# A filter fold that reads its mirrored half by a negative step, and a new fixed order of work

## The chip, the cores and the metric

The kernel runs on one core of one Trainium2 chip. The metric is the device time of one execution in microseconds (us), the median over repeated runs; the smaller the better. Besides it there is a profile of one execution of the kernel before: every instruction with its start and duration on each engine, what it waited for, and the transfers.

The engines by their short names: PE is TensorE (matmul), PEld its weight loads, DVE is VectorE, ACT is ScalarE, POOL is GpSimd, SP is SyncE, which issues most transfers. PE writes its results into PSUM, which has eight banks of 512 columns of 32 bits; DVE or ACT read them from there.

## What is computed

A gated sum of two branches over S = 2048 tokens of D = 640 features, all in bfloat16 at the borders:

```python
def _A_ref(q, k, v, shift_k, ssm_k, ssm_D):
    k_shift = sum of four shifted copies of k, each times its tap of shift_k
    kv = k_shift * v
    y = causal convolution of kv with the filters ssm_k, S long, by FFT over 2 * S
    y = y + kv * ssm_D
    return q * y

def _B_ref(x, w1, w2, w3, w4):
    h = gelu(layernorm(x) @ w1)
    hs = (quarters of h shifted by +1, -1, +2, -2 tokens) @ w2
    x1 = x + hs
    return x1 + gelu(layernorm(x1) @ w3) @ w4

x = A_q
g = sigmoid((x * gate_w).sum(-1, keepdims=True))
return g * _A_ref(x, A_k, A_v, ...) + (1 - g) * _B_ref(x, ...)
```

The code above is shortened to what each line computes.

## The kernel before

**Stages.** Tokens are the 16 tiles of 128 (t), or four chunks of 512 (sc). Branch B: `ln1` normalises the tiles of x and transposes them (tiles 0 to 7 by PE and an ACT copy, the others by a transposing transfer), `mm1` multiplies by w1 and applies Gelu on ACT, `mm2` multiplies by w2 and adds x, `ln2` normalises again and transposes, `mm3` multiplies by w3 with Gelu, `mm4` by w4. Branch A works on two halves of the features (g or hh) and four blocks of tokens (b or c): `kv_half` and `kv_block` make the products of k, taps and v on DVE and fold them, `x_fwd` takes their folded transform on PE, `h_load`, `h_fold` and `h_chunk` do the same for the filters in five chunks of 128 features, `unit` multiplies the spectra on DVE, and `final` transforms back, in 16 steps that are numbered k = 0 to 15 (first the eight of one half, then those of the other). Each `final` step has an inverse transform on PE, a copy on ACT, an addition and a subtraction on DVE, a flip of the difference by a matmul, a copy of the flipped half on ACT scaled by the gate, a product with q on DVE, and an output transfer, which either adds into memory (by POOL's queue) or is issued by SP after one more addition on DVE.

**The fold of the filters** (`h_fold`, L765 to L774). The real transform of 512 values needs the sums and the differences of value n and value 512 - n. `kst` holds four blocks of 512 values per feature. Before, ACT copies values 511 to 257 in reversed order into `krev` (L769), whose first column holds zeros (L708); DVE subtracts and adds 256 columns of four blocks (L770, L771) and puts value 256 into column 0 of the sums (L772). Two transposing transfers follow (L773), and `h_chunk` uses their results as matmul operands.

**The order of work.** The program first records all operations in a list (`P.op`, `P.dma`), with what each reads and writes; the number of an operation is its place there, 0 to 1300. `SEQUENCE` (L502) lists these numbers in the order in which they are to be issued; filtered by engine it is each engine's program. `schedule` (L271) goes through it with planned durations, gives each PSUM tile the bank that comes free first by that plan, and lets large transfers wait for an earlier transfer that the plan has finished. `emit` (L322) then places the semaphore waits that the data and the banks need. An engine works strictly in its list's order, so an instruction that waits holds up everything behind it on its engine.

**Lines that the profile names.** Helpers record most operations, so many have one line: L689 is every matmul of `mm`, L669 every two-operand instruction of `tt`, L674 every `ts` (a tensor with one or two scalars), L679 every `act`, L861 POOL's power in the layernorms, L857 and L858 the statistics of `ln1`, L903 the PE transposes of `ln1`, L237 every transfer. L715 is a row of 15 matmuls on ones that warms PE up at the start. L718 is one Gelu of a single column whose result nobody reads. L737 copies the parts of w1 for the last feature tile (w1x) and needs both halves of w1, which SP loads by two transfers (L733 to L735; operations 34 and 35). `ln2` of a tile runs POOL, POOL, DVE, POOL (the power), DVE in turn.

Of the kernel before, what the change touches and what calls it, by code (L numbers as in the profile page):

```python
# [173 lines left out]
class Prog:  # L174
# [96 lines left out]
    def schedule(self, sequence, backlog=3000.0):  # L271
        ops = self.ops
        delays = self.edges()
        free = {"pe": 1580.0, "act": 720.0, "dve": 930.0, "pool": 1190.0, "sp": 720.0}
        dfree = 0.0
        done = []
        avail = [0.0] * 8
        tenant = [None] * 8
        todo = {t.idx: len(t.users) for t in self.banks}
        last = {t.idx: 0.0 for t in self.banks}  # L280
        order = []
        for i in sequence:
            o = ops[i]
            st = max([free[o.eng]] + [ops[p].end + d for p, d in delays[i]])
            if o.nbytes and not o.tp and not o.early:
                st = max(st, dfree - backlog)
            t = o.tile
            if t is not None and t.place is None:
                free_at = {b: max(avail[b:b + t.n]) for b in range(0, 8, t.n)}
                st = max(st, min(free_at.values()))  # L290
                assert st < 1e17, "no bank"
                t.place = min((avail[b ^ 1] <= st if t.n == 1 else False, a, b) for b, a in free_at.items() if a <= st)[2]
                for b in range(t.place, t.place + t.n):
                    if tenant[b] is not None:
                        for u in tenant[b].users:
                            if ops[u].eng != "pe":
                                o.preds.setdefault(u, False)
                    tenant[b] = t
                    avail[b] = 1e18
            o.start = st  # L300
            free[o.eng] = st + o.dur
            o.end = st + o.dur
            if o.nbytes:
                dfree = max(st + 0.5 * o.dur, dfree) + o.cost
                o.end = max(dfree, o.end) + o.lat
                if o.cost > 500 and not o.tp and not o.early:
                    gate = [(ops[d].end, d) for d in done if ops[d].end <= st]
                    if gate:
                        o.preds.setdefault(max(gate, key=lambda g: g[0])[1], False)
                done.append(i)  # L310
            if t is not None:
                todo[t.idx] -= 1
                last[t.idx] = max(last[t.idx], o.end)
                if todo[t.idx] == 0:
                    for b in range(t.place, t.place + t.n):
                        avail[b] = last[t.idx] + 195.0
# [147 lines left out]
def bass_gated_mix__ssm_conv_h3__mixer_s_mlp__prompt_kernel(  # L464
# [33 lines left out]
    def ps(n, cls):  # L498
# [3 lines left out]
    SEQUENCE = [2, 3, 10, 11, 12, 31, 6, 57, 8, 1, 13, 14, 15, 16, 17, 18, 19, 20, 21, 22, 23, 24, 25, 7, 9, 0, 4, 28, 5, 56, 29, 63, 58, 64,  # L502
# [684 lines left out]
```

## Time and profile before

| what | value |
|---|---|
| time, median of 3 runs | 236.11 us (235.93 to 236.24) |
| span of the profiled execution, first to last instruction | 233.8 us |
| what lies around the span, against the median | 2.3 us |
| PE busy | 221.1 us |
| DVE busy | 220.1 us |
| ACT busy | 170.3 us |
| POOL busy | 105.9 us |

The profiled execution's own time is its span and the few microseconds around it, in which the execution is started and ended. A row of the profile's groups reads: line, engine, operation, what it writes and reads with partitions x elements, the count; then busy us and the mean ns of one; then the engine's idle time just before these instructions and what ended most of it. In the timeline the first two numbers are the start and the time taken, and a bracket gives the idle time ahead and what ended it. In the chain of waits each row is a start, a duration, and the engine and line that the end of the program was waiting for at that time.

### The profile page before, as it was taken

What the parts mean: (1) busy time and instruction counts of PE and PEld (TensorE: products, weight loads), DVE (VectorE), ACT (ScalarE), POOL (GpSimd) and SP (SyncE); (2) the same over time, 40 slices, a digit from 0 to 9 for tenths busy, and PEclk for the clock granted to TensorE, in tenths of its full rate; (3) what the DMA queues carried; (4) which work ended last, traced back from release to release, by engine and by line L of the source; (5) the groups of instructions that cost most, each with busy time, mean ns of one, the idle gap of its engine ahead of it and who ended that gap; (6) DMA issues with size and microseconds to landing.
All of it is one profiled execution on the core that took longest, in us unless ns stands there. A gap on an engine that the chain in (4) does not pass through costs nothing.

```text
span 233.8 us, 4171 instructions
## 1 busy us (share of the span) xinstructions
PE 221.1 (95%) x1501; PEld 134.6 (58%) x1501; DVE 220.1 (94%) x402; ACT 170.3 (73%) x317; POOL 105.9 (45%) x122
## 2 busy tenths in 40 slices
PE   7999999989998999999999999999999999999960
PEld 2598665436554656544775456654666556776630
DVE  6998999999988999998999999999989999979994
ACT  2799699488796899769949897577655387288881
POOL 0330406274495801196376693246024332456870
PEclk9999999999999999999999999999999999999997
DMA  5999959898878999978638988999978987989998
GB/s 161 360 345 250 253 146 271 246 277 204 140 181 176 240 213 317 343 212 180 157 97 145 187 189 163 146 191 206 259 142 145 196 140 142 185 98 111 95 109 165
DMA packets 63785, 45.48 MB, mean 195 GB/s; under 512 B 28818, under 2 KB 59028, under 8 KB 63764
## 3 DMA queue, kind: packets, MB, share of 16 engines
q1 hardware_dynamic: 54748, 33.33, 55.2%
q0 software_dynamic: 8832, 11.80, 34.9%
q8 instruction: 12, 0.20, 0.3%
q10 hardware_dynamic: 184, 0.08, 0.1%
q14 instruction: 9, 0.07, 0.1%
HBM read 24.22 MB, written 6.55 MB: 132 GB/s over the span
## 4 chain that ended last, share of the span: by engine, by line
PE 45%; DVE 9%; POOL 3%; ACT 2%; issue 1%
PE PSall L689 45%; DVE arena L669 8%; ACT arena L679 2%; POOL arena L674 1%; POOL arena L861 1%; POOL arena L669 1%; DVE arena L959 0%; DVE arena L674 0%
## 5 line engine op out<-in xcount | busy, mean ns | idle before, releaser
L689 PE MATMUL PSall<-arena 128*128 128x320 bf16 (+5 forms) x1444 | 213.7, 307 | 5.3 <-DVE arena L669 2.4
L669 DVE TENSOR_TENSOR arena<-arena 128x640 bf16<-128x640 bf16 (+5 forms) x247 | 182.3, 793 | 3.0 <-ACT arena L679 1.9
L689 PEld LDWEIGHTS PSall<-arena 128*128 128x128 bf16 (+1 forms) x1444 | 130.5, 98 | 86.9 <-DVE arena L669 4.2
L679 ACT ACTIVATE arena<-PSall 128x512 bf16<-128x512 f32 (+6 forms) x189 | 107.7, 634 | 29.4 <-PE PSall L689 25.2
L679 ACT ACTIVATE arena<-arena 128x640 bf16<-128x640 bf16 (+4 forms) x62 | 42.2, 703 | 6.7 <-POOL arena L669 2.7
L861 POOL TENSOR_TENSOR arena<-arena 128x1 f32<-128x1 f32 (+1 forms) x26 | 29.3, 1128 | 31.9 <-DVE arena L674 31.5
L674 POOL TENSOR_SCALAR arena<-arena 128x1 f32<-128x1 f32 (+2 forms) x41 | 24.8, 608 | 34.7 <-DVE arena L959 12.0
L237 POOL DMA_DIRECT2D out_dram<-arena x28 | 30.5, 1197 | 20.5 <-ACT arena L679 15.0
L679 ACT ACTIVATE arena<-PSall,arena 128x640 bf16<-128x640 f32 (+1 forms) x32 | 20.6, 658 | 20.0 <-PE PSall L689 19.9
L237 POOL DMA_DIRECT2D arena<-arena x12 | 14.9, 1242 | 32.1 <-DVE arena L669 28.2
L674 DVE TENSOR_SCALAR arena<-arena 128x640 bf16<-128x640 bf16 (+2 forms) x49 | 14.4, 307 | 3.4 <-POOL arena L674 1.6
L857 DVE BATCH_NORM_STATS2 arena<-arena 128x6 f32<-128x320 bf16 x32 | 14.6, 479 | 2.0 <-DMA arena<-in_A_q_dram 1.7
L669 POOL TENSOR_TENSOR arena<-arena 128x1 f32<-128x1 f32 (+1 forms) x11 | 10.3, 943 | 2.9 <-DVE arena L674 2.5
L715 PE MATMUL PSall<-arena 128*128 128x512 bf16 x15 | 5.4, 536 | 1.6 <-DVE arena L711 1.6
L959 DVE SCALAR_TENSOR_TENSOR arena<-PSall,arena 128x640 bf16<-128x640 f32 x8 | 6.4, 808 | 0.1
L924 DVE TENSOR_SCALAR arena<-arena 32x256 bf16<-32x256 bf16 (+1 forms) x24 | 5.9, 244 | 0.5
L679 ACT ACTIVATE PSall<-PSall 128x640 f32<-128x640 f32 x8 | 5.6, 699 | 0.1
L715 PEld LDWEIGHTS PSall<-arena 128*128 128x128 bf16 x15 | 1.9, 132 | 4.6 <-issue 2.5
L903 PE MATMUL PSall<-arena 128*128 128x128 bf16 x40 | 3.6, 219 | 0.3
L718 ACT ACT_TABLE_LOAD x1 | 1.3, 1283 | 2.7 <-issue 2.7
L903 PEld LDWEIGHTS PSall<-arena 128*128 128x128 bf16 x40 | 2.4, 97 | 1.4 <-DVE arena L858 0.4
L858 DVE BATCH_NORM_AGGREGATE arena<-arena 128x2 f32<-128x12 f32 x16 | 3.0, 197 | 0.0
(24 smaller groups left out, 9.6 us busy)
## 6 DMA issues: line engine op xcount, KB each, us to landing
arena<-arena POOLq DMA_DIRECT2D x12, 640.0 KB, 6.3
arena<-in_A_k_dram SPq DMA_DIRECT2D x14, 400.0 KB, 4.1
arena<-in_A_q_dram SPq DMA_DIRECT2D x14, 320.0 KB, 6.9
out_dram<-arena POOLq DMA_DIRECT2D x20, 160.0 KB, 4.2
arena<-in_A_ssm_k_dram SPq DMA_DIRECT2D x5, 512.0 KB, 4.4
arena<-in_A_v_dram SPq DMA_DIRECT2D x16, 160.0 KB, 3.9
arena<-in_B_w_dram SPq DMA_DIRECT2D x1, 1920.0 KB, 8.8
out_dram<-arena SPq DMA_DIRECT2D x10, 160.0 KB, 3.7
```

What stands on the lines that cost most here:

```text
L237: fn = lambda e: e.dma_start(out, in_, **kw)
L669: P.op(eng, lambda e: e.tensor_tensor(o, real(a), real(b), op), [a, b], [o], dve_ns(o, [a, b], 2) if eng == "dve" else 500)
L674: P.op(eng, lambda e: e.tensor_scalar(o, real(a), s1, s2, op0=op0, **({} if op1 is None else {"op1": op1})), [a] + aps, [o], dve_ns(o, [a] ...
L679: P.op("act", lambda e: e.activation(real(o), real(a), f, bias=bias, scale=scale, **({"accum_out": accum} if accum is not None else {})), ...
L689: fns.append(lambda e, l=l, r=r, i=i: e.matmul(real(o), l, r, start=(i == 0), stop=(i == last)))
L715: P.op("pe", lambda e: e.matmul(real(pw), warm[:, 0:128], warm[:, 128:640], start=True, stop=True), [warm], [pw], 427.0 if i < 14 else 216.0)
L857: P.op("dve", lambda e, o=o, i=i: e.bn_stats(o, i), [i], [o], 400)
L858: P.op("dve", lambda e: e.bn_aggr(bna[:, t, :], bns[k]), [bns[k]], [bna[:, t, :]], 120)
L861: P.op("pool", lambda g: g.tensor_tensor(o, a, e, ALU.pow), [a, e], [o], dur)
L903: P.op("pe", [lambda e, c=c, pb=pb, xn=xn: e.transpose(real(pb)[:, 128 * c:128 * (c + 1)], xn[:, 128 * c:128 * (c + 1)], ident) for c in r ...
L924: P.op("dve", lambda e, o=hT[q, 4, c0:c0 + n], i=hx[q, :]: e.tensor_scalar(o, i, 1.0, None, op0=ALU.mult), [hx[q, :]], [hT[q, 4, c0:c0 + n ...
L959: P.op("dve", lambda e: e.scalar_tensor_tensor(x, real(pr), 1.0, x, op0=ALU.mult, op1=ALU.add, accum_out=st[1, 0][:, t:t + 1]), [pr, x], [ ...
```

## The change

`h_fold` loses its ACT copy and the buffer `krev` with its two zero fills. DVE's subtraction and addition now read `k[:, :, 511:256:-1]`, the same memory with a step of -1, and cover columns 1 to 255 of each block; one instruction copies values 256 and 0 into column 0 of sums and differences. The operations number 1294 instead of 1301, so numbers in the new lists are up to seven lower than before for the same operation.

The order is a new one throughout. `schedule` no longer plans with durations: `PLACES` gives the bank of each of the 230 PSUM tiles, and `GATES` lists 63 pairs of operations, of which the first waits for the second. The planned duration of a DVE instruction with a negative step is no longer set apart (`dve_ns`), but the new `schedule` doesn't use planned durations.

The diff, with most of the lists cut. Operations that the text below names are, before and after: the one-column Gelu 26 and 24; the halves of w1 34 and 35, now 32 and 33; the second load of x tiles 4 to 7 142, now 140; ln2 of token tile 3 on DVE 441 and 443, now 434 and 436; subtraction and product of output step 2 1159 and 1162, now 1152 and 1155, and of output step 0 1137 and 1140, now 1130 and 1133.

```diff
@@ -268,52 +268,23 @@
             out.append(row)
         return out
 
-    def schedule(self, sequence, backlog=3000.0):
+    def schedule(self, sequence, places, gates):
         ops = self.ops
-        delays = self.edges()
-        free = {"pe": 1580.0, "act": 720.0, "dve": 930.0, "pool": 1190.0, "sp": 720.0}
-        dfree = 0.0
-        done = []
-        avail = [0.0] * 8
         tenant = [None] * 8
-        todo = {t.idx: len(t.users) for t in self.banks}
-        last = {t.idx: 0.0 for t in self.banks}
         order = []
+        for d, g in gates:
+            ops[d].preds.setdefault(g, False)
         for i in sequence:
             o = ops[i]
-            st = max([free[o.eng]] + [ops[p].end + d for p, d in delays[i]])
-            if o.nbytes and not o.tp and not o.early:
-                st = max(st, dfree - backlog)
             t = o.tile
             if t is not None and t.place is None:
-                free_at = {b: max(avail[b:b + t.n]) for b in range(0, 8, t.n)}
-                st = max(st, min(free_at.values()))
-                assert st < 1e17, "no bank"
-                t.place = min((avail[b ^ 1] <= st if t.n == 1 else False, a, b) for b, a in free_at.items() if a <= st)[2]
+                t.place = places[t.idx]
                 for b in range(t.place, t.place + t.n):
                     if tenant[b] is not None:
                         for u in tenant[b].users:
                             if ops[u].eng != "pe":
                                 o.preds.setdefault(u, False)
                     tenant[b] = t
-                    avail[b] = 1e18
-            o.start = st
-            free[o.eng] = st + o.dur
-            o.end = st + o.dur
-            if o.nbytes:
-                dfree = max(st + 0.5 * o.dur, dfree) + o.cost
-                o.end = max(dfree, o.end) + o.lat
-                if o.cost > 500 and not o.tp and not o.early:
-                    gate = [(ops[d].end, d) for d in done if ops[d].end <= st]
-                    if gate:
-                        o.preds.setdefault(max(gate, key=lambda g: g[0])[1], False)
-                done.append(i)
-            if t is not None:
-                todo[t.idx] -= 1
-                last[t.idx] = max(last[t.idx], o.end)
-                if todo[t.idx] == 0:
-                    for b in range(t.place, t.place + t.n):
-                        avail[b] = last[t.idx] + 195.0
             o.order = len(order)
             order.append(o)
         return order
@@ -499,70 +470,88 @@
-    SEQUENCE = [2, 3, 10, 11, 12, 31, 6, 57, 8, 1, 13, 14, 15, 16, 17, 18, 19, 20, 21, 22, 23, 24, 25, 7, 9, 0, 4, 28, 5, 56, 29, 63, 58, 64,
-                59, 27, 141, 30, 60, 35, 61, 52, 65, 62, 76, 66, 26, 80, 67, 34, 77, 42, 68, 78, 70, 146, 53, 82, 69, 71, 43,
-                44, 46, 83, 79, 48, 50, 73, 81, 142, 321, 72, 47, 144, 301, 74, 75, 96, 205, 98, 86, 97, 84, 39, 87, 36, 143,
...
-                677, 655, 660, 647, 623, 441, 442, 702, 289, 290, 291, 292, 704, 652, 276, 424, 653, 656, 414, 443, 284, 705,
...
-                1187, 1075, 1108, 1061, 1173, 1110, 1107, 1079, 1120, 1158, 1159, 1143, 1160, 1161, 1132, 1174, 1076, 1137,
-                1080, 1138, 1139, 1149, 1062, 1177, 1178, 1109, 1162, 1111, 1140, 1070, 1081, 1150, 1188, 1189, 1125, 1163,
...
+    SEQUENCE = [1, 6, 27, 8, 9, 10, 0, 2, 11, 12, 13, 55, 28, 61, 62, 63, 66, 67, 57, 78, 29, 14, 15, 54, 58, 59, 16,
+                77, 25, 60, 56, 71, 64, 17, 79, 18, 139, 141, 19, 20, 72, 21, 22, 23, 26, 73, 40, 41, 42, 33, 144,
+                82, 140, 50, 51, 145, 75, 3, 44, 46, 45, 146, 65, 32, 48, 102, 68, 69, 299, 74, 98, 76, 80, 34, 49,
...
+                610, 327, 225, 259, 227, 234, 235, 236, 631, 634, 654, 360, 333, 341, 230, 635, 434, 435, 629, 237,
...
+                372, 714, 294, 417, 730, 705, 734, 436, 733, 570, 735, 736, 292, 293, 757, 454, 710, 715, 571, 295,
...
+                1150, 1009, 1124, 1159, 1160, 1161, 1021, 1028, 1147, 1096, 1042, 24, 1085, 1089, 1053, 1015, 1126,
...
+                1165, 1130, 1072, 1104, 1166, 1167, 1073, 1142, 1074, 1143, 1075, 1106, 1105, 1107, 1054, 1055, 1151,
+                1152, 1056, 1153, 1144, 1131, 1145, 1118, 1057, 1114, 1115, 1154, 1155, 1170, 1171, 1172, 1173, 1174,
+                1181, 1182, 1132, 1203, 1133, 1183, 1175, 1176, 1184, 1204, 1192, 1193, 1156, 1205, 1177, 1178, 1185,
...
+    PLACES = [6, 3, 1, 0, 2, 5, 6, 3, 6, 4, 6, 5, 7, 3, 4, 4, 3, 7, 4, 0, 0, 7, 6, 7, 1, 0, 0, 5, 1, 4, 3, 0, 5, 1,
...
+    GATES = [(299, 26), (318, 140), (247, 202), (592, 39), (600, 318), (593, 318), (599, 36), (31, 38), (337, 592),
+                (248, 31), (624, 337), (623, 337), (630, 324), (631, 225), (654, 225), (360, 225), (655, 225),
...
+                (1168, 883), (1124, 591), (1053, 591), (1065, 1099), (1071, 1111), (1257, 1211), (1267, 1200)]
...
@@ -610,7 +599,6 @@
     kv_rev = [V(o, 640).rearrange("p (s d) -> p s d", s=2) for o in (oKV + 7040, oPT + 2560)]
     kpr = V(oPT, 2560).rearrange("p (s j d) -> p s j d", s=2, j=4)
     kst = [V(oXF + 10240 + 2048 * i, 2048).rearrange("p (b n) -> p b n", b=4) for i in range(2)]
-    krev = [V(oXF + 14336 + 1024 * i, 1024).rearrange("p (b n) -> p b n", b=4) for i in range(2)]
     het = [V(oXF + 16384 + 2048 * i, 2048).rearrange("p (e b k c) -> p e b k c", e=2, b=4, k=2) for i in range(2)]
     kfo = [V(oW3 + 2048 * i, 2048).rearrange("p (e b n) -> p e b n", e=2, b=4) for i in range(2)]
     xT = [V(oXT + 2560 * i, 2560).rearrange("p (c s) -> p c s", c=5) for i in range(3)]
@@ -659,8 +647,6 @@
 
     def dve_ns(o, i, mode):
         n = n_of(o)
-        if any(x[0] < 0 for a in i for x in list(a.ap)[1:]):
-            mode = 1
         if is_ps(o) or any(is_ps(a) for a in i):
             return n / 0.96 + 150
         return n / (0.96 * mode) + 65
@@ -704,8 +690,6 @@
     P.op("dve", lambda e: e.memset(hT[64:96, 4, 2:4], 0.0), [], [hT[64:96, 4, 2:4]], 70)
     P.op("dve", lambda e: e.memset(hT[32:64, 4, S + 1:S + 2], 0.0), [], [hT[32:64, 4, S + 1:S + 2]], 70)
     P.op("dve", lambda e: e.memset(hT[96:128, 4, S:S + 2], 0.0), [], [hT[96:128, 4, S:S + 2]], 70)
-    for i in range(2):
-        P.op("dve", lambda e, i=i: e.memset(krev[i][:, :, 0:1], 0.0), [], [krev[i][:, :, 0:1]], 70)
     WARM = 15
     const("warm")
     P.op("dve", lambda e: e.memset(V(oUT + 2048, 640), 1.0), [], [V(oUT + 2048, 640)], 230)
@@ -764,12 +748,11 @@
 
     def h_fold(c):
 
-        k, kr, fo = kst[c % 2], krev[c % 2], kfo[c % 2]
+        k, fo = kst[c % 2], kfo[c % 2]
         tt(k[:, 0, 0:1], k[:, 0, 0:1], Dcol[:, c:c + 1], ALU.add)
-        act(kr[:, :, 1:256], k[:, :, 511:256:-1], ACTF.Copy)
-        tt(fo[:, 1], k[:, :, 0:256], kr, ALU.subtract)
-        tt(fo[:, 0], k[:, :, 0:256], kr, ALU.add)
-        ts(fo[:, 0, :, 0:1], k[:, :, 256:257], 1.0, None, ALU.mult)
+        tt(fo[:, 1, :, 1:256], k[:, :, 1:256], k[:, :, 511:256:-1], ALU.subtract)
+        tt(fo[:, 0, :, 1:256], k[:, :, 1:256], k[:, :, 511:256:-1], ALU.add)
+        ts(fo[:, :, :, 0], k.rearrange("p b (h n) -> p h b n", h=2)[:, ::-1, :, 0], 1.0, None, ALU.mult)
         for e in range(2):
             P.dma(sp, het[c % 2][:, e].rearrange("p b k c -> p (b k) c"), fo[:, e].rearrange("p b n -> p (b n)"), transpose=True)
 
@@ -1153,7 +1136,7 @@
             for q in range(2):
                 at(final, hh, c, q, 8 * hh + 2 * (3 - c) + q)
 
-    sched = P.schedule(SEQUENCE)
+    sched = P.schedule(SEQUENCE, PLACES, GATES)
     with nc.Block() as block:
         P.emit(block, sched)
 
```

125 rows, old and new, of tables (GATES, PLACES, SEQUENCE) are left out of this document.

## The prediction

> **What bounds the kernel now.** I read the page's totals first, then the costliest groups, then the table by stretches, then the chain of waits, and last the list of who waited for whom.
>
> ```profile
> span 233.8 us, 4171 instructions
> PE 221.1 (95%) x1501; PEld 134.6 (58%) x1501; DVE 220.1 (94%) x402; ACT 170.3 (73%) x317; POOL 105.9 (45%) x122
> ...
> L689 PE MATMUL PSall<-arena 128*128 128x320 bf16 (+5 forms) x1444 | 213.7, 307 | 5.3 <-DVE arena L669 2.4
> ```
>
> Two engines are nearly full: PE is idle for 12.7 us of the span and DVE for 13.7 us. The last row says that only 5.3 us of PE's idle time stands in front of its real matmuls. A busy PE need not be a fast one, so I checked the long middle stretch by the table by stretches (from:to and length, then busy us and instructions of PE, its weight loads, DVE, ACT and POOL, the granted clock, the DMA share and GB/s), by the matmul groups in it and by the chain of waits.
>
> ```profile
> 0.00:10.00 10.00, 8.23 (x47) 3.72 (x47) 7.13 (x33) 4.11 (x8) 2.36 (x8) 1.00 0.81 235
> 10.00:20.00 10.00, 9.87 (x161) 8.81 (x159) 9.31 (x31) 9.69 (x30) 2.27 (x5) 1.00 1.12 352
> ...
> 106.60:150.00 43.40, 43.39 (x272) 26.50 (x273) 42.08 (x51) 34.67 (x61) 26.21 (x25) 1.00 0.77 159
> 150.00:208.60 58.60, 58.60 (x372) 36.13 (x371) 57.04 (x56) 35.20 (x60) 19.98 (x20) 1.00 0.91 171
> 208.60:222.00 13.40, 13.03 (x95) 8.82 (x92) 12.76 (x28) 11.90 (x23) 9.81 (x9) 1.00 0.96 104
> 222.00:233.80 11.80, 4.23 (x27) 2.33 (x27) 8.44 (x27) 5.79 (x12) 4.77 (x4) 0.88 0.94 137
> ```
> ```profile
> L689 PE MATMUL PSall<-arena 128*128 128x320 bf16 x457 | 64.8, 299 | 0.0
> L689 PE MATMUL PSall<-arena 128*128 128x512 bf16 x185 | 42.5, 379 | 0.3 <-ACT arena L679 0.3
> ```
> ```profile
> 106.61 102.03 PE PSall L689 x640
> ...
> 208.66 0.54 ACT arena L679
> ...
> 228.51 1.91 DVE arena L669 x7
> ...
> 230.45 0.32 DVE arena L669
> ```
>
> From 106.6 to 208.6 the chain is PE alone. 457 matmuls of 320 columns and 185 of 512 are 240,960 columns; 102.03 us over them is 0.42 ns a column, at a granted clock of 1.00. No gap is left there, so PE cannot pass that stretch faster; it can only reach it sooner. DVE is 97% busy in the same stretch (99.1 of 102 us). From 208.6 on the chain is almost all DVE, whose last instruction ends at 230.77; 3.0 us follow for the last output transfers. So the end is set by two full engines that hold each other up: what can be won is their waits, and what DVE gets to do more is paid. DVE's waits, and PE's longest, stand in the list of waits (total us, times, longest):
>
> ```profile
> PE PSall L689 <- DVE arena L669: 2.4, 3, 1.8
> ...
> DVE arena L669 <- ACT arena L679: 1.9, 3, 0.7
> DVE arena L857 <- DMA arena<-in_A_q_dram: 1.7, 3, 0.7
> DVE arena L674 <- POOL arena L674: 1.6, 2, 1.1
> DVE arena L674 <- ACT arena L679: 1.2, 2, 1.0
> DVE arena L674 <- POOL arena L861: 0.5, 1, 0.5
> DVE arena L737 <- DMA arena<-in_B_w_dram: 0.4, 1, 0.4
> ```
>
> DVE's come to 7.3 us: 2.1 are waits for loads in the head, which an order of instructions does little about, and 5.2 waits for ACT and POOL, which an order can shift.
>
> **The fold.** Per filter chunk (five of them) the change removes one reversed copy on ACT and leaves two subtract/add instructions on DVE, now 128x1020 with one operand read backwards and both outputs starting at an odd element. The copy of column 256 goes from 4 to 8 elements.
>
> ```profile
> L669 DVE TENSOR_TENSOR arena<-arena 128x2560 bf16<-128x2560 bf16 x68 | 98.4, 1485 | 0.2
> L669 DVE TENSOR_TENSOR arena<-arena 128x1280 bf16<-128x1280 bf16 x44 | 35.2, 818 | 0.8 <-ACT arena L679 0.7
> L669 DVE TENSOR_TENSOR arena<-arena 128x1024 bf16<-128x1024 bf16 x10 | 6.7, 680 | 0.0
> ...
> L679 ACT ACTIVATE arena<-arena 128x1020 bf16<-128x1020 bf16 x5 | 5.3, 1065 | 2.6 <-DMA arena<-in_A_ssm_k_dram 2.5
> ```
>
> ACT loses 5 x 1.065 = 5.3 us, two of them inside the stretch 10 to 20 us where it is 97% busy. ACT is 73% busy over the span and is in the chain only in short pieces, so I credit nothing directly; the relief pays for an addition below.
>
> DVE: between 1280 and 2560 elements a two-operand instruction costs (1485 - 818) / 1280 = 0.52 ns an element. No row shows one that reads backwards. If that is free, each of the ten costs 680 ns less four elements: no change. If the engine then falls to half its rate per element, each gains 1020 x 0.52 = 0.53 us, ten of them 5.3 us, on the engine that has no room. Below nothing there is no gain, since the instruction has the same count of elements. The nearest rows speak for the low end. ACT read the same columns backwards at 1065 ns for 1020 elements, its ordinary pace (its 128x1024 copies out of PSUM take 1026 ns). And the copies of 32 rows by 256, half of which write at an odd column, show no second speed (shortest, median and longest ns):
>
> ```profile
> L924 DVE TENSOR_SCALAR arena<-arena x24: 200/223/291, 13.2 to 75.2; 32x256 bf16<-32x256 bf16 x16, 32x512 bf16<-32x512 bf16 x8
> L679 ACT ACTIVATE arena<-PSall 128x1024 bf16<-128x1024 f32 x16 | 16.2, 1026 | 1.6 <-PE PSall L689 1.2
> ```
>
> I take 0 and keep 5.3 for the range. [...]
>
> The two removed zero fills of the reversed buffer lie in DVE's idle time before its first load arrives, and give nothing. But the new order moves four of the eight other fills from there into the full stretch (places 22, 40, 60 and 176 among DVE's instructions):
>
> ```profile
> L708 DVE MEMSET arena<- 128x4 bf16 x2 | 0.1, 62 | 0.1
> ```
>
> 4 x 62 ns = **+0.25 us** on DVE.
>
> **The head.** The new order moves two things to the worse there.
>
> ```profile
> 2.73 1.28 ACT L718 ACT_TABLE_LOAD   x1 [2.73 <-issue]
> ...
> 4.03 0.20 ACT L718 ACTIVATE arena<-arena 128x1 bf16<-128x1 bf16 x1
> ...
> 7.16 2.00 ACT L679 ACTIVATE arena<-PSall 128x10 bf16<-128x10 f32 x4 [2.93 <-PE PSall L752]
> ```
>
> The dummy Gelu of L718 (operation 26 before, 24 after) draws the table load into 2.73 to 4.03 us, where ACT has nothing to do until 7.16. In the new order it is ACT's 233rd operation, beside mm3 of the last 512 tokens, and ACT's first arithmetic is a plain Copy. So a table for Gelu is loaded in front of the first real Gelu, about 9 to 10 us into the span, while the evictions of the first normalised tiles are due: between 0 (if ACT waits for PE there anyway) and 1.28 us. Behind it queue the Gelu evictions that free PSUM and the evictions of transposed tiles that PE waits for. [...] The price of 1.28 us is the trace's.
>
> Second, the two halves of w1 (operations 34 and 35, now 32 and 33) are no longer issued back to back: the second load of x tiles 4 to 7 (142, now 140) goes between them. It moves 320 KB; at the 345 to 360 GB/s of the second and third slices of the span that is 0.9 us.
>
> ```profile
> GB/s 161 360 345 250 253 146 271 246 277 204 140 181 176 240 213 317 343 212 180 157 97 145 187 189 163 146 191 206 259 142 145 196 140 142 185 98 111 95 109 165
> ...
> 10.00 0.33 DVE L737 TENSOR_SCALAR arena<-arena 128x640 bf16<-128x640 bf16 x1 [0.43 <-DMA arena<-in_B_w_dram]
> ```
>
> w1 is late already: DVE waited 0.43 us for it at 10.0. It will be there at about 10.9; until then PE has the warm-up, the taps, two transposed tiles and one part of mm1, and then waits; on DVE the w1x copy of L737 has two more instructions and a fill ahead of it than before, so DVE waits less than that, but what follows it waits with it. Bounds 0 and 0.9 us. The table load falls under the same 0.9 us and ACT has 2.1 us less to do afterwards, so the two do not add: I take **+0.7 us** together.
>
> **The order.** For DVE's 5.2 us I compared where each waiting instruction stands in the two orders, counting instructions between it and what it waits for.
>
> ```profile
> 69.03 0.21 DVE L674 TENSOR_SCALAR arena<-arena 128x1 f32<-128x1 f32 x1 [1.13 <-POOL arena L674]
> 69.21 1.49 DVE L669 TENSOR_TENSOR arena<-arena 128x2560 bf16<-128x2560 bf16 x1
> 71.16 0.45 DVE L674 TENSOR_SCALAR arena<-arena 128x640 bf16<-128x640 bf16 x1 [0.46 <-POOL arena L861]
> ...
> 207.46 1.23 DVE L669 TENSOR_TENSOR arena<-arena 128x640 bf16<-128x640 bf16 x2 [0.72 <-ACT arena L679]
> 209.22 3.03 DVE L669 TENSOR_TENSOR arena<-arena 128x640 bf16<-128x640 bf16 x4 [0.54 <-ACT arena L679]
> ```
>
> The first three rows are ln2 of token tile 3 (441 and 443): one instruction of 1.49 us stands between its two DVE steps while POOL computes the power. In the new list (434 and 436) 70 instructions stand there. The last two rows are the flipped halves of output steps 2 and 0 (1162 and 1140): two and three instructions stand behind their subtraction, four and twelve in the new order (1155, 1133). The other waits are loosened alike: ln2 of tile 11, which cost the 1.0 us for ACT, is later on DVE while the eviction it waits for is earlier on ACT. So each of the 5.2 us that can move does so; an order that closes old waits opens others, and the tail has one that looks tighter (between subtraction and product of output step 4 a 128x640 product takes the place of a 128x1280 one). I count two thirds, **-3.5 us**. PE's 5.3 us must shrink with it; its largest wait, the 1.8 us in the tail, is for DVE and goes when DVE is early.
>
> **Sum.** 233.8 + 0 (fold) + 0.25 (fills) + 0.7 (head) - 3.5 (order) = 231.25 us of span. The runs shown have a median of 236.11, so 2.3 us lie around the span of the profiled execution; with them **233.6 us**, 1.1% faster. Its own range: all 5.2 us won and the head free, 231.2; only 1.5 us won, 235.6.
>
> **The rivals.**
> A, slower: DVE takes the backward or odd-element operands at half rate. For it: no row shows such a read by DVE, and DVE has no slack. Against it: the ACT and odd-column rows above. Price 5.3 us: 233.6 + 5.3 = 238.9, a little less where a fold falls into one of DVE's waits for loads, say 238.5. It decides from 0.25 us an instruction on.
> B, slower: the fold is free, but the order wins nothing net, because fixed banks and a plan that no longer follows its own times put new waits (for a PSUM bank, for POOL) in place of the old 5.2 us, and the head still costs its part: 236.1 + 0.95 = 237.1. For it: PE's waits are also for evictions (the 0.3 us for ACT ahead of mm3), and every bank is newly placed; against it: the distances counted above.
> C, no change: the order wins about 1 us and the head costs as much: 236.1.
>
> **Chances.** Forecast 0.58, A 0.11, B 0.21, C 0.10. A measurement of this kernel tells a change from none at about 0.2%, 0.5 us. Faster 0.58, within 0.2% 0.10, slower 0.32. The range must hold B and most of A: 231.0 to 238.6.
>
> **What would show it.** The ten fold instructions at 0.68 us (A: 1.2). Two table loads, the second near 9 to 10 us, and a PE wait of up to 1.5 us there. DVE's waits for ACT and POOL together under 2 us instead of 5.2, and the 102 us of unbroken PE beginning some 2.5 us earlier than 106.6. If the span is longer though the folds take 0.68 us, my reading of the order is wrong; if DVE's waits shrink and the time does not, PE's own waits have taken their place.

## The result and the profile after

| kernel | median | runs | ratio to before, 95% interval |
|---|---|---|---|
| before | 236.02 us | 235.21 to 236.24 | |
| after | 247.62 us | 245.88 to 253.78 | 1.0471 (1.0423 to 1.052) |

The changed kernel is 4.7% slower, 11.6 us where 2.5 us less were forecast. One of its four runs, of 253.78 us, was in a slow state, with a mean granted clock of 0.963 against 0.972 to 0.977 in the others; the other three have a median of 247.07, 11.1 us above before, and below such runs are left out of every difference to before. The profiled execution took 248.18 us with a span of 246.4, so 1.8 us lie around the span. The page's totals, columns as before:

```profile
span 246.4 us, 4148 instructions
PE 226.2 (92%) x1501; PEld 135.7 (55%) x1501; DVE 220.8 (90%) x400; ACT 168.9 (69%) x313; POOL 109.8 (45%) x122
```

Both full engines have as much work as before (DVE 220.8 against 220.1 us). PE's 5.1 us more are no more work: its clock is lower in places, as the table by stretches shows (columns as in the prediction, the clock third from the end):

```profile
80.00:90.00 10.00, 9.99 (x62) 5.72 (x60) 9.93 (x21) 7.76 (x11) 0.75 (x1) 1.00 0.88 148
90.00:100.00 10.00, 6.69 (x32) 3.35 (x33) 7.55 (x16) 4.38 (x8) 4.82 (x7) 0.80 1.08 284
100.00:110.00 10.00, 10.00 (x44) 4.46 (x43) 8.29 (x13) 5.98 (x12) 4.03 (x7) 0.86 0.90 208
150.00:160.00 10.00, 7.07 (x40) 4.22 (x39) 9.71 (x10) 5.30 (x10) 3.30 (x4) 0.87 1.07 180
160.00:170.00 10.00, 10.00 (x61) 5.87 (x59) 8.81 (x9) 5.12 (x9) 6.70 (x8) 0.96 1.01 190
```

The fold is in the groups by shape, the waits in the list of waits:

```profile
L655 DVE TENSOR_TENSOR arena<-arena 128x1020 bf16<-128x1020 bf16 x10 | 6.8, 678 | 0.4 <-DMA arena<-in_A_ssm_k_dram 0.4
L665 ACT ACT_TABLE_LOAD x2 | 2.6, 1283 | 2.8 <-issue 2.8
```
```profile
ACT arena L665 <- DMA out_dram<-arena: 8.3, 2, 4.4
...
DVE arena L655 <- ACT arena L665: 6.2, 6, 2.8
...
PE PSall L675 <- DMA arena<-in_B_w_dram: 4.5, 2, 3.2
PE PSall L675 <- ACT arena L665: 3.8, 2, 2.9
...
DVE arena L660 <- ACT arena L665: 2.8, 2, 1.5
...
DVE arena L942 <- PE PSall L675: 2.1, 1, 2.1
```

The fold runs at 678 ns, against 680 before: the backward read costs nothing here. Two waits are new and one has grown: ACT waits 8.3 us for two output stores, PE 3.2 us for a load of weights, and DVE's waits for ACT went from 3.1 to 9.0 us. The chain of waits says where they lie:

```profile
85.22 4.00 DMA arena<-in_A_k_dram
89.92 7.23 DMA arena<-in_B_w_dram
97.24 13.81 PE PSall L675 x54
...
117.28 4.15 POOL arena L844
...
149.96 1.13 SPq L234
151.14 4.35 DMA out_dram<-arena
155.57 0.80 ACT arena L665
156.42 76.64 PE PSall L675 x482
```

The unbroken PE stretch of the chain, 102.03 us from 106.61 before, now begins at 156.42. Two transfers stand in the chain ahead of it.

- **The w3 load.** Its two issues (operations 522 and 523) went out at 85.5 and 78.0 us before and go out at 87.1 and 89.9 now. The first matmul of `mm3` stands ready near 94 us and starts at 97.24, 7.2 us after the second issue.
- **The base stores.** `base` writes a token tile of X to the output (L975 of the changed kernel); `mm4` then writes its own result over that tile of X, so its ACT copy has to wait until the store has read it. Stores 6 and 5 (operations 969 and 963) were issued at 117.7 and 138.5 us before, 39 and 13 us ahead of those copies. Now they are issued at 151.1 and 159.2, behind other work in SP's queue, though their data was ready at 147.0 and 126.7. ACT comes to the two copies at 151.7 and 160.0, less than 1 us after the issues. The timeline has the two waits, and PE's behind the first, whose next PSUM bank is the one that the waiting copy holds. The second is not the store's alone: the matmuls of mm4-5 that the copy reads end at 162.2, so 2.2 of its 4.4 us are left to the store, and PE does not wait behind it:

```profile
151.14 1.21 SPq L237 DMA_DIRECT2D out_dram<-arena  x1
...
155.57 0.79 ACT L665 ACTIVATE arena<-PSall,arena 128x640 bf16<-128x640 f32 x1 [3.87 <-DMA out_dram<-arena]
...
156.42 9.83 PE L675 MATMUL PSall<-arena 128*128 128x320 bf16 x57 [2.93 <-ACT arena L665]
...
164.41 0.79 ACT L665 ACTIVATE arena<-PSall,arena 128x640 bf16<-128x640 f32 x1 [4.43 <-DMA out_dram<-arena]
```

To add it up I took from the traces what PE loses: the time from the start of one real matmul to the next, less what the first takes at full clock (136 ns for 320 columns, 216 ns for 512, as in undisturbed stretches). Start, loss and the time behind the last matmul leave 213 us of work in each kernel:

| us | first real matmul | lost to 20 us | 20 to 90 | 90 to 130 | 130 to 210 | 210 to last matmul | behind it | span |
|---|---|---|---|---|---|---|---|---|
| before | 6.9 | 1.2 | 3.3 | 0.4 | 0.1 | 3.2 | 5.4 | 233.8 |
| after | 7.0 | 2.7 | 2.0 | 7.5 | 4.8 | 2.3 | 7.0 | 246.4 |
| e_w3_base | 6.9 | 3.1 | 2.9 | 2.4 | 0.0 | 2.3 | 7.0 | 237.5 |
| e_mix | 7.0 | 2.4 | 2.1 | 1.5 | 5.4 | 2.3 | 7.0 | 240.5 |
| e_yield | 7.0 | 1.9 | 1.7 | 2.2 | 0.0 | 2.3 | 6.9 | 234.7 |

(The last three are experiments below.) Up to 90 us the new order is no worse than the old: it loses 1.5 us more in the head and 1.3 less afterwards. 11.8 of the 12.6 us of span come between 90 and 210 us.

### The profile page after: what moved, and what is told of

It reads as the page before. It is cut to its first block, busy times and chain, and to the rows that moved or that the text cites. A ratio compares the mean times of both kernels' runs of the same rounds, so it can differ in the third digit from the quotient of the medians.

```text
span 246.4 us, 4148 instructions
## 1 busy us (share of the span) xinstructions
PE 226.2 (92%) x1501; PEld 135.7 (55%) x1501; DVE 220.8 (90%) x400; ACT 168.9 (69%) x313; POOL 109.8 (45%) x122
## 4 chain that ended last, share of the span: by engine, by line
PE 45%; DVE 27%; DMA 13%; ACT 5%; issue 4%; SPq 3%; POOL 2%; DVEq 0%; ACTq 0%
PE PSall L675 45%; DVE arena L655 17%; DMA arena<-in_B_w_dram 6%; ACT arena L665 5%; DVE arena L840 3%; DMA arena<-in_A_k_dram 3%; DVE arena L660 3%; SPq L237 2%; DMA arena<-in_A_ssm_k_dram 2%; DVE arena L907 2%; DMA out_dram<-arena 2%; POOL arena L844 2%; DVE arena L942 1%; SPq L234 1%; DVE arena L841 1%
## 5 line engine op out<-in xcount | busy, mean ns | idle before, releaser
L675 PE MATMUL PSall<-arena 128*128 128x320 bf16 (+5 forms) x1444 | 218.7, 311 | 10.9 <-DMA arena<-in_B_w_dram 4.5
L655 DVE TENSOR_TENSOR arena<-arena 128x2560 bf16<-128x2560 bf16 (+5 forms) x247 | 183.5, 793 | 9.2 <-ACT arena L665 6.2
L844 POOL TENSOR_TENSOR arena<-arena 128x1 f32<-128x1 f32 (+1 forms) x26 | 36.3, 1396 | 35.1 <-DVE arena L660 34.7
L665 ACT ACTIVATE arena<-arena 128x640 bf16<-128x640 bf16 (+3 forms) x57 | 36.9, 672 | 5.1 <-POOL arena L655 3.4
L237 POOL DMA_DIRECT2D out_dram<-arena x28 | 31.2, 1139 | 18.8 <-ACT arena L665 12.8
L660 POOL TENSOR_SCALAR arena<-arena 128x1 f32<-128x1 f32 (+2 forms) x41 | 23.3, 570 | 35.8 <-DVE arena L841 13.6
L665 ACT ACTIVATE arena<-PSall,arena 128x640 bf16<-128x640 f32 (+1 forms) x32 | 20.4, 655 | 19.6 <-PE PSall L675 11.1
L655 POOL TENSOR_TENSOR arena<-arena 128x1 f32<-128x1 f32 (+1 forms) x11 | 8.7, 788 | 3.2 <-DVE arena L660 2.6
L699 PE MATMUL PSall<-arena 128*128 128x512 bf16 x15 | 6.1, 581 | 1.9 <-DVE arena L695 1.9
```

The costliest lines, as they stand in the source:

```text
L237: fn = lambda e: e.dma_start(out, in_, **kw)
L655: P.op(eng, lambda e: e.tensor_tensor(o, real(a), real(b), op), [a, b], [o], dve_ns(o, [a, b], 2) if eng == "dve" else 500)
L660: P.op(eng, lambda e: e.tensor_scalar(o, real(a), s1, s2, op0=op0, **({} if op1 is None else {"op1": op1})), [a] + aps, [o], dve_ns(o, [a] ...
L665: P.op("act", lambda e: e.activation(real(o), real(a), f, bias=bias, scale=scale, **({"accum_out": accum} if accum is not None else {})), ...
L675: fns.append(lambda e, l=l, r=r, i=i: e.matmul(real(o), l, r, start=(i == 0), stop=(i == last)))
L699: P.op("pe", lambda e: e.matmul(real(pw), warm[:, 0:128], warm[:, 128:640], start=True, stop=True), [warm], [pw], 427.0 if i < 14 else 216.0)
```

## The experiments

Theory 1: transfers are issued too late for their users in the new order. Rivals: the fixed PSUM banks (2), the fold (3), the fixed waits of transfers, `GATES` (4). Names are those of the program: ln2-13 is `ln2` of token tile 13, mm4-5 `mm4` of tile 5. Each kernel was timed beside the kernel before on the same chip, and "+4.4" is a median less that of before in the same runs; after stands at +11.1.

**The fold alone, and the order alone.** Both are put together from the two kernels:

```diff
 e_fold: h_fold, L751 to L757, as after
-    SEQUENCE, PLACES, GATES = after's
+    SEQUENCE, PLACES, GATES = before's order, banks and waits
 e_order: SEQUENCE, PLACES, GATES as after, and in h_fold
-        tt(fo[:, 1, :, 1:256], k[:, :, 1:256], k[:, :, 511:256:-1], ALU.subtract)
+        act(kr[:, :, 1:256], k[:, :, 511:256:-1], ACTF.Copy)
+        tt(fo[:, 1], k[:, :, 0:256], kr, ALU.subtract)
```

> The order, the banks and the waits of the kernel before; only the fold is the new one (VectorE reads the mirrored half backwards, no reversed ScalarE copy, no zero fills; two of the one-instruction column copies stand a little earlier). Theory 1 (late transfers of the new order: the w3 load and the base stores) lets the fold cost nothing: 236.0 us, between 235.0 and 236.8, the folds at 0.68 us each. Theory 2 (banks and gates): the same 236. Theory 3 (the fold, or what ScalarE does in its place, costs the time): 243 to 248 us.

> The order, the banks and the gates of the changed kernel, with the old fold put back (five reversed ScalarE copies of about 1.2 us, each right ahead of its fold, and the two zero fills). Theory 1: the loss is all the order's: 247 to 250 us, with the 3.2 us wait of TensorE for the w3 load and the two waits of ScalarE of about 4 us for the base stores still there. Theory 2: the same. Theory 3: 236 to 239 us.

Measured: e_fold 235.23 us, ratio 0.9972 (0.9942 to 1.0002); e_order 255.14, ratio 1.0829 (1.0781 to 1.0878), +19.5. Theory 3 falls: the fold costs nothing. Run once more (e_fold2, below) it gave 0.998 (0.9952 to 1.0008). The order alone is slower than both changes together by 8.4 us, more than theory 1 allowed. The waits of DVE's two-operand instructions for ACT are 12.7 us there instead of 6.2, 7.7 us of them ahead of three folds, and a step of DVE's statistics that the changed kernel does at 34.7 us comes at 42.7: the five copies hold the folds up, and what is queued behind them. So the new fold is worth some 8 us to this order, and nothing that can be told to the old one.

**The late transfers, one by one.**

```diff
 e_w3: SEQUENCE and GATES
-    ..., 756, ..., 757, ..., 522, ..., 523, ...   (522, 427), (523, 437)
+    ..., 522, 756, ..., 523, 757, ...
 e_base: SEQUENCE
-    ..., 521, ..., 569, ..., 969, ..., 963, ...
+    ..., 963, 521, ..., 969, 569, ...
 e_w3_base: both
```

> The changed kernel with the w3 load alone moved ahead (two SyncE issues, their two gates out). Theory 1: the wait of TensorE for w3 near 97 us and the half clock behind it go; TensorE lost 6.2 us between 90 and 110 us and loses 2.9 us between 80 and 100 us where the w3 load and the base stores were both moved, so 3.3 us less: 244.3 us (243 to 245.5). A rival: the TensorE time is given back at the base stores, which then come at the same time for an earlier use: less than 1 us, 246.6 or more.

> The changed kernel with the base stores 6 and 5 alone moved ahead in SyncE's queue. Theory 1: the two waits of ScalarE for them (3.9 and 4.4 us) go; TensorE lost 4.4 us behind the first of them, so 4.3 us less: 243.3 us (242 to 244.5), and together with the w3 load's part the two make the 7.6 us that both gave. The rival: less than 1 us.

> The changed kernel with four transfers moved ahead in SyncE's queue and nothing else: the two halves of the w3 load ahead of two key loads (issued near 75 and 81 us instead of 87 and 90, their two gates taken out), the base store 6 ahead of the ln2-13 transfer and the base store 5 ahead of the ln2-11 transfer. Theory 1: the 3.2 us wait for w3 with the 2.5 us of half clock behind it, and the waits of 3.9 and 4.4 us for the stores with theirs, are gone: 10 us less, 237 us (235 to 240). Theories 2 and 3: the waits are only the visible part, less than 3 us comes back: 244.5 or more.

Measured: e_w3 245.0 us (1.0363, 1.0302 to 1.0423), +8.4; e_base 243.23 (1.031, 1.0234 to 1.0386), +6.9; both 240.03 (1.0206, 1.0146 to 1.0266), +4.4. The gains are 2.7, 4.2 and 6.7 us, so they add up as theory 1 has it, but stay 3 us short of the 10 that I expected together; the interval of e_w3 only just leaves that of the changed kernel. A part went into a new wait, which is largest where the head is mended too:

**With the head mended.**

```diff
 e_all: SEQUENCE, besides e_w3_base
-    ..., 140, ..., 32, ...      24 among ACT's last
+    ..., 32, ..., 140, ...      24 behind ACT's five transfers at the start
```

> The w3 load and the two base stores moved ahead as before, and the head mended too: the dummy Gelu stands first on ScalarE behind its five transfers and the second half of the w1 load goes out right behind the first, ahead of a half of the x load. Theory 1: TensorE's stall of 1.4 us near 11 us for the second half of w1 goes: 238.6 us (237.8 to 239.6). The rival (something else bounds the head, such as VectorE's work on x): 239.7 to 240.5.

Measured: runs from 241.9 to 249.7 us, no ratio. The profiled one took 242.5, so both expectations are missed, upwards. PE's wait for w1 in the head is gone, and `mm1` starts at 10.5 us instead of 11.5 in e_w3_base. The time goes later, and not in the head where the rival looked for it; DVE and PE in the timeline:

```profile
87.39 0.44 DVE L665 TENSOR_SCALAR arena<-arena 128x640 bf16<-128x640 bf16 x1 [4.72 <-DMA arena<-arena]
...
89.67 1.55 PE L680 MATMUL PSall<-arena 128*128 128x320 bf16 x6 [4.49 <-DVE arena L660]
```

DVE waits 4.7 us for the transposing transfer of an `ln2` tile, which the earlier w3 load is now ahead of (3.7 us in e_w3, 2.0 in e_w3_base; in the changed kernel DVE's only wait for such a transfer is 1.2 us, at 97.98). So here one transfer moved ahead made another late.

**The cost put into the old order.** Both start from e_fold:

```diff
 e_late_base: SEQUENCE, GATES
+    963 behind 965, 969 behind 970;   (963, 965), (969, 970)
 e_late_w3: SEQUENCE
+    523 behind 477 (the ln2-7 transfer)
```

> The suspected cost put into the kernel that doesn't have it: the order of the kernel before with the new fold (235.2 us in e_fold), where the base stores 5 and 6 alone are held until the last, or the next to last, matmuls of mm4-5 and mm4-6 are done, some 3 to 5 us ahead of ScalarE's use of X as in the changed kernel. Theory 1: ScalarE waits about 4.4 us at mm4-5 and 2.5 to 4 us at mm4-6 for the stores, TensorE loses the 4 to 6 us that it lost in the changed kernel near 156 us: 239.2 to 241.5 us. The rival (the old order has cover for a late store, the new order's loss has another cause): 237 us or less.

> The order of the kernel before with the new fold, where the second issue of the w3 load alone stands behind the ln2-7 transfer in SyncE's queue (issued near 89 us instead of 77.5, with its first user on TensorE near 92 us). Theory 1: TensorE waits some 4 us for w3 (7 us from issue to landing), and loses 2 to 3 us more at half clock: 239 to 242 us. The rival: TensorE has slack here, since VectorE sets the pace up to about 90 us, and less than 1.5 us comes out: 236.7 or less.

Measured: e_late_w3 239.37 us (1.0154, 1.0115 to 1.0192), 4.4 us more than e_fold by the ratios' runs (+4.0 against -0.4): as theory 1 had it. Its table by stretches, behind a PE wait of 3.9 us:

```profile
95.13:100.20 5.07, 5.07 (x15) 2.11 (x15) 1.52 (x3) 1.42 (x3) 0.00 (x0) 0.51 1.08 352
100.20:106.00 5.80, 5.80 (x31) 2.89 (x30) 5.70 (x8) 3.83 (x8) 3.36 (x4) 1.00 0.57 166
```

PE runs 5 us at a clock of 0.51. e_late_base gave 236.52 (1.0058, 1.003 to 1.0087), +1.2, as the rival had it: 1.6 us more than e_fold. ACT waited 3.7 us, but once (the two stores went out together), and PE behind it 0.95 us. So one late store by itself costs little there; in the new order the same two are worth 4.2 us. There PE's next group needs the bank of the waiting copy; that this makes the difference was read from the trace and not tried.

**Banks and fixed waits.**

```diff
 e_nogates:  GATES = []
 e_banks:    PLACES = the banks that before's planner gives for this order
 e_plan:     schedule() of before: banks and waits from its planner
```

> The changed kernel with the order and the banks as they are and the list of fixed waits of transfers empty. Theory 1: SyncE still issues in the same order, so the base stores stay late; the w3 load comes 1 to 2 us earlier as with the planner's waits: 244 to 247 us. Theory 4 (the fixed waits alone cost the time): 241 us or less, and the wait for w3 gone. Against both: with nothing held back, bulk loads fill the rings ahead of the small transfers that are waited for: 248 us or more.

> The changed kernel with the order and the fixed waits as they are, and of the planner of the kernel before only its choice of PSUM banks (175 of 230 tiles get another bank). e_plan took both from that planner (242.5 us), e_nogates took the waits away (244.1 us) against 247.6. Theory 1: the banks are worth 1.1 +- 1 us, 246.5 us (245.5 to 248), and the stalls for w3 and the base stores are still there. Theory 2 (the fixed banks carry the loss): 243 or less.

> The new fold and the new order, but PSUM banks and the waits of transfers come from the planner of the kernel before, not from the two fixed lists. Theory 1 (what stands where in SyncE's queue): the transfers stand as late as in the changed kernel, so 245 to 250 us. Theory 2 (the fixed banks, or the fixed waits, cost the time): 235 to 240 us.

Measured: e_nogates 244.13 us (1.0312, 1.0238 to 1.0386), +7.8; e_banks 244.58 (1.0408, 1.0372 to 1.0444), +9.5; e_plan 242.53 (1.0264, 1.0211 to 1.0317), +6.8. The first is as theory 1 had it; the other two lie below theory 1's ranges and e_plan above theory 2's as well. Against +11.1 the waits are worth 3.3 us, the banks 1.6 (their interval overlaps that of the changed kernel), both together 4.3. So neither list carries the loss, but they are not nothing: without the waits the second w3 issue goes out 1.1 us earlier (88.8) and PE waits 1.7 instead of 3.2 us; with other banks one wait of 4.1 us for a store is left of two.

**A new loss, and what it is.**

```diff
 e_nogates_base: e_base with GATES = []
 e_mix: e_nogates_base, e_all's head, and in SEQUENCE
+    522, 523 ahead of 763
```

> The changed kernel without its list of fixed waits and with the base stores 6 and 5 moved ahead. Without the list the wait for w3 was 1.8 us instead of 3.2 and no half clock followed; e_nogates gave 3.5 us and e_base 4.4. Theory 1: the two are different stalls and add up: 239.7 us (238.7 to 241). The rival (both are the same time, given back once): 242 or more.

> As e_nogates_base, with the head of e_all (dummy Gelu first, the halves of w1 back to back) and both halves of the w3 load one right behind the other some 2.5 us earlier, ahead of the third key load of kv_block-1-2 instead of behind it. Theory 1: the 1.8 us wait for w3 and about 1 us of the head's stall go: 237 us (236 to 238.5). The rival, as in e_all: the earlier w3 load stands in the rings ahead of the small transposing transfers of ln2, VectorE waits for these, and 239 us or more come out.

Measured: e_nogates_base 246.55 us (1.0455, 1.0423 to 1.0488), +11.2; e_mix 243.24 (1.0318, 1.0285 to 1.0351), +7.9. Both miss, upwards. In e_nogates_base PE still waits 2.8 us for the w3 load; in e_mix the waits aimed at are gone (the table above), but PE loses 5.4 us near 184. POOL's timeline in e_mix, and the same place in e_w3_base:

```profile
170.73 8.81 POOL L842 TENSOR_TENSOR arena<-arena 128x1 f32<-128x1 f32 x1 [0.17 <-DVE arena L658]
179.62 1.08 POOL L653 TENSOR_TENSOR arena<-arena 128x1 f32<-128x1 f32 x1
```
```profile
173.43 1.73 POOL L849 TENSOR_TENSOR arena<-arena 128x1 f32<-128x1 f32 x1 [0.68 <-DVE arena L665]
```

One power of one element per partition, that of `ln2` of tile 14, takes 8.8 us instead of 1.7 (8.8 in e_nogates_base too, 1.7 in the changed kernel). DVE begins eleven two-operand instructions at 170.56, most of 128x2560, without a gap for 14.3 us, and ACT waits 6.4 us for `ln2` of tile 14. The next kernel has one wait more: DVE's next instruction waits for POOL.

```diff
 e_yield: e_mix, SEQUENCE and GATES
+    576, 577, 578, ...    GATES = [(1080, 578)]
 e_yield2: the same for ln2-11
+    517, 518, 519, ...    GATES = [(1080, 578), (833, 519)]
```

> e_mix with one wait more and nothing else: the VectorE instruction behind the one that releases GpSimd's power operation for the row block ln2-14 waits until GpSimd has done that block's two operations. In e_mix this power operation of one element per partition took 8.8 us beside eleven VectorE instructions in a row, against 1.7 us in the changed kernel, and TensorE lost 5.4 us behind it near 184 us. Theory 5 (GpSimd's small operation doesn't get through while VectorE runs pairs of operands without a break): the power operation takes 0.6 to 1.8 us, TensorE's 5.4 us shrink below 1, VectorE's 1 to 2 us of idleness cost little there: 238.5 us (237.5 to 240) against 243.2. The rival (ScalarE's late block has another cause, such as the transfer ahead of it): 242.5 or more.

> As e_yield, and the same wait for the row block ln2-11, whose power operation took 4.1 us near 111 us with two TensorE stalls of 0.4 and 0.9 us behind it. Theory 5: another 0.5 to 1 us less than e_yield, 237.8 us (236.8 to 239.2). The rival: VectorE is the bound there, and its idleness costs as much as it gives: the same as e_yield or up to 1.5 us more.

Measured: e_yield 237.0 us (1.0078, 1.0053 to 1.0102), +1.9; e_yield2 237.19 (1.0086, 1.0052 to 1.0121), +2.1. POOL and DVE in e_yield's timeline:

```profile
170.26 0.56 POOL L842 TENSOR_TENSOR arena<-arena 128x1 f32<-128x1 f32 x1 [0.18 <-DVE arena L658]
170.89 0.19 POOL L653 TENSOR_TENSOR arena<-arena 128x1 f32<-128x1 f32 x1
171.12 19.91 DVE L653 TENSOR_TENSOR arena<-arena 128x2560 bf16<-128x2560 bf16 x15 [0.95 <-POOL arena L653]
```

0.95 us of DVE's time buys 6 us, somewhat more than expected. Theory 5 is shown for this place. The other run does not test its place, since its expectation names the wrong block. By the order of POOL's program the operation of 4.1 us is that of ln2-8, while that of ln2-11 took 0.74 us in e_yield. POOL in e_yield2, ln2-8 and then ln2-11:

```profile
109.74 4.14 POOL L842 TENSOR_TENSOR arena<-arena 128x1 f32<-128x1 f32 x1 [2.03 <-DVE arena L658]
...
116.38 0.57 POOL L842 TENSOR_TENSOR arena<-arena 128x1 f32<-128x1 f32 x1 [1.06 <-DVE arena L658]
```

The long one stands there unchanged. It stands in the changed kernel's chain too (4.15 us at 117.28; ln2-8 took 0.79 us before), and what it costs stays open.

**The tail.** PE now loses no more than before (8.1 against 8.2 us, from the table's e_yield and before), and what is left is behind the last matmul. GpSimd's last store before and after:

```profile
227.14 1.20 POOL L237 DMA_DIRECT2D out_dram<-arena  x1 [0.15 <-issue]
```
```profile
239.77 1.21 POOL L237 DMA_DIRECT2D out_dram<-arena  x1 [0.47 <-DVE arena L655]
```

Each span ends 6.6 to 6.7 us behind it.

```diff
 e_tail: e_yield, SEQUENCE (and the bank of one tile)
-    1244, ... 1245, ... 1246, 1247, ... 1235, 1236, 1237, 1238
+    1244, 1235, ... 1245, 1236, ... 1246, 1237, 1247, 1238
```

> e_yield with output step 10 finished right behind step 11 (its last TensorE, ScalarE, VectorE instruction and its accumulating store on GpSimd's queue), ahead of steps 12, 13 and 8 instead of behind them; four tiles of these steps get other PSUM banks. In the profiles of four kernels the span ends 6.6 to 6.7 us after GpSimd's last store is issued (227.14 to 233.8 before, 239.77 to 246.4 in the changed kernel, 226.73 to 233.4 in e_fold, 228.14 to 234.7 in e_yield). If that store sets the end, it is issued 1.3 to 1.7 us earlier and 1.4 us come out: 235.6 us (234.9 to 236.3) against 237.0. The rival (VectorE's last 13 instructions, or SyncE's stores, set the end): 236.6 or more.

> The same kernel as e_fold (the order before with the new fold) once more, beside e_tail on the same chip. Expected: 0.5 us below the kernel before, ratio 0.998 (0.995 to 1.000), and faster than or equal to e_tail.

Measured: e_tail 236.74 us (1.0047, 1.0014 to 1.008), +0.9; e_fold2 235.52 (0.998, 0.9952 to 1.0008), -0.3. e_tail is 1.0 us below e_yield against before, but the two intervals overlap, and 236.74 lies above the expected range. That GpSimd's last store sets the end is not shown: in e_tail's trace it lands at 232.0 us, and SyncE's last store, issued at 229.8, only at 232.9, so the rival may hold. No version beats the kernel before beyond the interval; the fold in the old order comes nearest.

## Why the prediction was wrong

The predicted 233.6 us (231.0 to 238.6) missed by 14 us.

- **The fold, 0: right.** 678 ns against 680; the bound of 5.3 us and rival A are out. The half rate behind both was my assumption; no run shows it.
- **The fills, 0.25:** too small to be told.
- **The head, 0.7: right in its marks.** Two table loads, at 2.8 and 10.8 us, the second forecast for 9 to 10, and PE's and DVE's waits for the second half of w1. That a second load would come was my inference: before has one. PE loses 1.5 us more up to 20 us; what this is worth at the end was not separated.

```profile
10.82 1.28 ACT L665 ACT_TABLE_LOAD   x1
11.32 0.33 DVE L721 TENSOR_SCALAR arena<-arena 128x640 bf16<-128x640 bf16 x1 [1.19 <-DMA arena<-in_B_w_dram]
11.34 1.01 PE L675 MATMUL PSall<-arena 128*128 128x128 bf16 x15 [1.27 <-DMA arena<-in_B_w_dram]
```

- **The order, -3.5: this step failed,** in sign and size. I counted the instructions between each *old* wait and what it waited for, found every distance longer, and credited two thirds of 5.2 us. DVE's waits for ACT and POOL, forecast under 2 us together, are 9.5. Those for POOL did shrink, from 2.1 to 0.5 us, and PE's loss from 20 to 90 us fell from 3.3 to 2.0. Those for ACT are 9.0 us. 3.9 of them (2.8 and 1.1) stand behind ACT's waits for the stores and are gone in e_base; 2.8 are `ln2` of tiles 9 and 11, and 2.1 are output steps of the tail. Tile 11 I had counted as loosened from both sides, and its wait grew; before and after:

```profile
107.79 0.22 DVE L674 TENSOR_SCALAR arena<-arena 128x1 f32<-128x1 f32 x1 [1.01 <-ACT arena L679]
```
```profile
123.63 0.21 DVE L660 TENSOR_SCALAR arena<-arena 128x1 f32<-128x1 f32 x1 [1.23 <-ACT arena L665]
```

  So a place in one engine's list does not say when the other engine comes to its own. And the count left out what had no wait before because it was early: SP's queue. There the w3 load's lead over its first matmul fell from 6.9 us (85.5 to 92.4) to some 4, and the base stores' lead over ACT's copies from 39 and 13 us to less than 1 us ahead of the time at which ACT came to them. Moving these four transfers ahead gives 6.7 us.
- **Rival B had the kind, not the size.** New waits took the old ones' place, but I gave it 237.1 us: no more than the 5.2 us given back. Nothing limits what a late transfer costs to what the order could win. Fixed lists, my reason for B, carry 1.6 us (banks, not clear of noise), 3.3 us (waits of transfers) and 4.3 us (both) in experiments of their own, which overlap with the late transfers.
- **The range** held no case in which one transfer comes late and PE loses its clock as well (0.51 for 5.6 us behind the w3 load).

So 6.7 of the 11.1 us are shown to go with the four late transfers. e_yield, where besides the head is mended, the w3 load stands in another place and the fixed waits are left out, is at +1.9. How the rest divides among these was not separated, since each changes when the others come. The long wait behind POOL at ln2-14 is no part of it: in the changed kernel that operation takes 1.7 us.

## What to carry to other kernels

When an order is replaced, check every transfer's lead over its first user and over the first writer of what it reads, above all those that never waited: that lead does not show among the waits of the old profile. An operation that was off the chain (a store that frees a buffer) set the time here, when the instruction behind it held the bank that the full engine needed next: ACT's 3.9 us for the store became 2.9 us of PE's. And mend one late transfer at a time and look again, since an earlier one may only pass the delay on, as the 4.7 us in e_all.

## What had not been expected of the hardware

**PE's clock fell after some pauses.** The stretches behind the two PE waits in the changed kernel:

```profile
97.24:102.80 5.56, 5.56 (x16) 2.19 (x17) 2.75 (x5) 1.19 (x2) 0.98 (x1) 0.51 1.14 248
102.80:108.40 5.60, 5.60 (x29) 2.71 (x28) 4.79 (x8) 3.62 (x7) 3.05 (x7) 1.00 0.75 151
156.42:160.60 4.18, 4.18 (x19) 2.52 (x20) 3.89 (x4) 2.81 (x6) 2.70 (x3) 0.61 0.89 178
```

A wait of 3.2 us is followed by 5.6 us at a granted clock of 0.51, so it costs 2.7 us more; the second wait, of 2.9 us, by 4.2 us at 0.61, which is some 1.6 more. In e_late_w3 5.1 us at 0.51 follow a pause of 3.9 us, and in e_all a clock between 0.7 and 0.8 in the 6 us from 90.2 follows one of 4.5 us. But the clock stayed at 1.00 behind pauses of 2.8 and 2.0 us in e_mix and one of 1.7 us in e_nogates, so of two pauses of nearly one length, 2.8 and 2.9 us, one was followed by a low clock and one was not. In the changed kernel's record of the clock the two low stretches last 6.8 us, from 95.9, its first 1.3 us in the pause, and 3.4 us, from 157.3, 0.9 us behind the pause. What decides it was not shown.

**One small operation of POOL took 8.8 us beside DVE's products.** In e_mix that is about six of DVE's products at 1.48 us; in e_yield, where DVE paused for 0.95 us, the operation took 0.56, and in the changed kernel 1.7. What keeps it waiting was not shown; the runs show that one small GpSimd operation stood beside some six of DVE's products in a row.
